# The second softmax's scores as eight small matmuls at once, and its transposes moved from TensorE to VectorE

## The chip, the cores and the metric

The kernel runs on one core of a Trainium2 chip. The metric is the device time of one launch, in microseconds, from runs of the same program. TensorE (PE in the profile; PEld is its weight load) writes only to PSUM. VectorE (DVE) and ScalarE (ACT) do the elementwise work, SyncE's queue (SP) starts most transfers and GpSimd's (POOL) a few. Each engine works through its own queue in order and waits at an instruction whose inputs or buffers aren't ready.

## The reference, cut to what matters

For 8 batches, 8 heads, 576 queries and keys of 64 values, and 32 packed rows per head:

```python
def sm_attn(qq, kk, vv):
    s = scale * np.matmul(qq, kk.transpose(0, 1, 3, 2))
    s = s - np.max(s, axis=-1, keepdims=True)
    a = np.exp(s)
    a = a / (np.sum(a, axis=-1, keepdims=True) + 1e-09)
    return np.matmul(a, vv)
p_packed = sm_attn(p, k, v)
out = sm_attn(q, p_packed, p_packed)
```

`out`, as 4608 tokens of 512 values, then goes through two MLPs with hidden size 2048. The first has a piecewise square as its nonlinearity, the second has SiLU. The change concerns the second `sm_attn`: its scores have 576 queries against 32 packed keys, per head, and its softmax runs over those 32.

## The kernel before, in words

The kernel is one program in two parts: attention with the first MLP (part A), then the second MLP (part B). Part A is a list of 256 steps, 32 for each of the 8 batches: 16 hidden blocks for each of the two halves (288 queries) of a batch. In each step TensorE does `a_h` for the step four ahead (line 569, six matmuls of 288 columns into one PSUM bank `ps_h`) and `a_y` for the step itself (line 604, twelve matmuls). Between them, over the steps in between, ScalarE makes `u` from `ps_h` (lines 578 and 579), VectorE limits it (`a_max`, line 584), ScalarE rounds it to `g` (line 588) and VectorE makes the rest of `g` (`a_lo`, line 594), one step ahead of the `a_y` that reads it. After the 16 steps of a half, `a_y`'s results are copied out by both (lines 613 and 616).

The output of the second softmax is not multiplied by the packed values on its own. The packed rows are multiplied into `w_in` first (`wp8`, line 497; `wp_out` casts it, lines 150 and 151), and `a_h` multiplies that with the softmax `a2`. So `a2`, with the (head, packed row) pairs on the partitions and queries along the free dimension, as a rounded part and a rest, is all that the second softmax has to deliver.

All work is put into one list of events with a key each, sorted, and emitted in that order, which is then the order of every engine's queue. Step i's `a_h` has key i + 0.3, its `a_y` i + 0.9, and the jobs of attention stand between them at i + 0.6. For batch b from 2 on, attention is done during the 32 steps of the batch before; the first of them is called `base` in the code. `front` (first softmax, packed rows) begins at `base` + 2, `back` (second softmax) at `base` + 14, `wp8` at `base` + 21, 25, 29 and 33, each with `wp_out` a step later. The new `a2` is wanted by `a_h` from `base` + 28 on.

`back` before: the 576 queries are taken as two tiles of 256 and one of 64, four steps apart. Each goes through six jobs, a step apart. `s2` (line 420) uses queries as weights, 64 at a time, and moves the 64 columns of packed keys of two heads: 16 matmuls, 4 for the last tile, which put queries on the partitions and the 32 packed rows of each head side by side. `s2_sub` (lines 431, 433) and `s2_norm` (446 to 449) are the softmax on VectorE around ScalarE's exponential `s2_exp` (438). `s2_tr` (457) turns the result with TensorE, against an identity, into PSUM, and `s2_out` (477, 479) splits it into `a2`.

Line 275 (`s1_8`) and line 286 (`s1_end8`) of `front`, and `wp8`, have a form that matters below: eight matmuls with 64 rows of contraction and 32 columns of weights, on eight tiles of TensorE's array, with 512 columns moving; results of the two heads of a pair go to two banks.

The preparation of the second MLP's weights is spread over the same steps: every 25 steps two conversions on VectorE (`conv_b`, lines 168 and 169) and then `a_first` to `a_fourth` (lines 651 to 660 with 151). For batch 4 (`base` 96) they fall on `base` + 17 and 19, and + 21 to 24.

The banks `ps_h`, `ps_s`, `ps_tr`, `ps_wp` come from one pool of four. Large SBUF tiles come from one pool, `big`, of 37.

Of the kernel before, what the change touches and what calls it, by code (L numbers as in the profile page):

```python
# [74 lines left out]

@with_exitstack
def attention_then_two_mlps(ctx: ExitStack, tc: tile.TileContext, kT, vv, qT, pT, w_in, w_out, w2_in, w2_out, out):

    nc = tc.nc
    B, P, NJ, S = kT.shape
    NP = pT.shape[3]
    D = P // 2
# [6 lines left out]
    HB = S // 2  # L102
    SC = S // P
    ST = S - SC * P
    NG = NJ // 2
# [8 lines left out]
    scale = 1.0 / float(D) ** 0.5  # L114

    const = ctx.enter_context(tc.tile_pool(name="const", bufs=1))
    big = ctx.enter_context(tc.tile_pool(name="big", bufs=37))
# [3 lines left out]
    a2_p = a2_s.enter_context(tc.tile_pool(name="a2_p", bufs=1))  # L121
    tc.swap_default_side()
    att = att_s.enter_context(tc.tile_pool(name="att", bufs=1))
# [10 lines left out]
    pb = const.tile([P, NJ, N2], F32, name="pbd")  # L134
# [11 lines left out]
    def bank(name):  # L146
        return ps_h.tile([P, 512], F32, tag="h", name=name)
# [6 lines left out]
    def words_of(raw):  # L154
        return raw.bitcast(U32).rearrange("p (n t) -> p n t", t=2)

    def to_f32_begin(raw):

        high = words_of(raw)[:, :, 1].bitcast(F32)
        nc.scalar.activation(high, high, AF.Prelu, scale=2.0 ** -112, alpha=-(2.0 ** 32))  # L162
# [25 lines left out]
    def conv_a(key):  # L188
        to_f32_begin(raw_t[key])
# [22 lines left out]
    kq_t, v_t, a2_t, wp_t = {}, {}, {}, {}  # L212
# [15 lines left out]
    def q_tiles(b):  # L228

        if b:  # L230
            return [[(2 * i * P, P), ((2 * i + 1) * P, P)] for i in range(SC // 2)] + [[(SC * P, ST)]]
        return [x for t in (0, HB) for x in ([(t, P), (t + P, P)], [(t + 2 * P, HB - 2 * P)])]

    def load_q(b, i):
        parts = q_tiles(b)[i]
        n = sum(x[1] for x in parts)
        if n > ST:
            t = big.tile([P, NJ, n], F32, tag="big", name="qt")
        else:
            t = att.tile([P, NJ, n], F32, tag="kqe", name="qte", bufs=2)  # L240
        nc.sync.dma_start(t, qT[b, :, :, parts[0][0]:parts[0][0] + n])
        kq_t["q", b, i] = t
# [9 lines left out]
    def att_jobs(b):  # L252


        st = {}
        pp = pp_t[b % 2]
# [148 lines left out]
        W2 = NJ * N2  # L405

        tiles = q_tiles(b)

        def s2(i):
# [53 lines left out]
        def s2_out(i):  # L463
# [14 lines left out]
            for hi, low, src in pieces:  # L478
                nc.vector.tensor_tensor(low, src, hi.bitcast(F32), op=ALU.subtract)

        def wp(f, g):
            ps = bank("ps_wp")
            w = w_in_t[g, f]
            for jj in range(2):
                nc.tensor.matmul(  # L485
                    ps[jj * N2:(jj + 1) * N2, :FW], pp[:, 2 * g + jj, :], w[:, jj, :], start=True, stop=True
                )
            st["wp", f, g] = ps
# [21 lines left out]
        def J(fn, *a):  # L510
            return lambda: fn(*a)
# [17 lines left out]
            [J(pp_out)],  # L529
        ]  # L530

        def back(every=4, only=None):
            which = range(len(tiles)) if only is None else only
            jobs = [[] for _ in range((len(which) - 1) * every + 6)]
            for n, i in enumerate(which):
                for k, fn in enumerate((s2, s2_sub, s2_exp, s2_norm, s2_tr, s2_out)):
                    jobs[n * every + k].append(J(fn, i))
            return jobs

        wps = [  # L540
            [[J(wp, f, g) for g in range(NG)] if b < 2 else [J(wp8, f)], [J(wp_out, f, g) for g in range(NG)]]
            for f in range(NF)
        ]
        return front, back, wps

    win_t = {}
# [74 lines left out]
    def load_part(b, t):  # L621
        for d in range(0, KD, 2):
            ysb = wk.tile([P, 2, HB], F32, tag="ysb", name="ysb", bufs=2)
            nc.sync.dma_start(ysb, y_dram[:, d:d + 2, t, b * HB:(b + 1) * HB])
            part_t["y", d // 2] = ysb

    def split_a(p, w, j, step):
# [168 lines left out]
                    s0 += m  # L804


    G = dict(pf1=4, pb1=18, w1=2, pf=2, pb=14, pw=21, lw=3, lk=4, lv=-1, lq=6, ai=34, ad=25, bev=4, oraw=1)
    starts = {b: (0,) if b else (0, KF // 2) for b in range(B)}
    steps = []
    for b in range(B):  # L810
# [6 lines left out]
    def ev(key, fn, *args):  # L817
        events.append((key, len(events), fn, args))

    def at(n, fn, *args):  # L820
        ev(n + 0.6, fn, *args)
# [4 lines left out]
    def slots(n, jobs, every=1):  # L826
        for i, slot in enumerate(jobs):
            for fn in slot:
                at(n + i * every, fn)

    with tc.manual_schedule():
# [3 lines left out]
        for _ in range(10):  # L835
            nc.tensor.matmul(warm[:, :P], ident, ident, start=True, stop=True)
        front, back, wps = att_jobs(0)

        def fill(n, own):
# [36 lines left out]
        def W(f, k, g):  # L876
            return (f"W{f}.{k}.{g}", wps[f][k][g])
# [67 lines left out]
        for g in range(NG):  # L945
            for k in range(2):
                n, fn = W(1, k, g)
                job(n, 2 + 0.1 * k + 0.01 * g, fn)
        for f in range(2, NF):
            for g in range(NG):  # L950
                for k in range(2):
                    n, fn = W(f, k, g)
                    job(n, 4 * f + k + 0.6, fn)
        for i, key in enumerate(ins[2 * KD:]):
            n = i + 3
# [54 lines left out]
        for p in range(NPR):  # L1010
            n = G['ai'] + G['ad'] * p
# [18 lines left out]
        for i in range(NBK):  # L1030
            n = kb(i * NPR)
# [92 lines left out]
```

## Time and profile before

| | |
|---|---|
| median of 3 runs | 1531.75 us (1530.99 to 1532.3) |
| span of the profiled execution | 1530.2 us |
| PE busy | 1512.8 us, 99% |
| PEld busy | 1380.4 us, 90% |
| DVE busy | 875.1 us, 57% |
| ACT busy | 743.4 us, 49% |
| POOL busy | 85.3 us, 6% |

The runs' time is that of the whole launch; the span runs from the first to the last instruction of one profiled execution. Busy times are shares of that span. Part A ends near 785 us.

### The profile page before, as it was taken

Reading aid. Unit: us, or ns where it says so; the run is one execution under the profiler, and the core shown is the slowest. Engines: PE = TensorE matmul, PEld = TensorE weight load, DVE = VectorE, ACT = ScalarE, POOL = GpSimd, SP = SyncE. Lnnn points to the kernel's source line nnn. Section 1 sums busy time; section 2 is a strip of 40 time slices with the busy share of each in tenths; the row PEclk is TensorE's granted clock in tenths of the full one; section 3 lists DMA queues with packets and bytes.
Section 4 is the critical chain, followed back from the end, with each engine's and each line's share of the span. In section 5 each row is a group of like instructions: output and inputs, shape, how many; then the busy total and the mean of one; then the engine's idle time right before and its main releaser. Section 6 shows DMA issues by size and latency. Waiting matters only on the chain.

```text
span 1530.2 us, 27671 instructions
## 1 busy us (share of the span) xinstructions
PE 1512.8 (99%) x10546; PEld 1380.4 (90%) x10546; DVE 875.1 (57%) x1831; ACT 743.4 (49%) x1665; POOL 85.3 (6%) x132
## 2 busy tenths in 40 slices
PE   8999999999999999999999999999999999999998
PEld 6788999989899899999998989999898989899997
DVE  5886565564746555575666664564364456447343
ACT  4775657565665656666754442343243334224232
POOL 1430000000000000000000010010001001001000
PEclk9999999999999999999999999999999999999999
DMA  9564545252445252432255653535444445445341
GB/s 333 178 222 141 187 132 169 100 166 102 139 157 169 89 182 70 167 116 92 99 179 187 214 165 108 175 122 161 138 137 146 136 147 160 123 151 173 103 138 62
DMA packets 136723, 226.99 MB, mean 148 GB/s; under 512 B 24336, under 2 KB 70416, under 8 KB 136592
## 3 DMA queue, kind: packets, MB, share of 16 engines
q1 hardware_dynamic: 127120, 192.19, 38.5%
q0 software_dynamic: 9472, 33.04, 6.6%
q8 instruction: 84, 1.38, 0.4%
q14 instruction: 47, 0.39, 0.1%
HBM read 186.25 MB, written 38.93 MB: 147 GB/s over the span
## 4 chain that ended last, share of the span: by engine, by line
PE 92%; DVE 2%; ACT 1%; issue 0%; DMA 0%; SPq 0%; DVEq 0%; ACTq 0%
PE ps_o L784 26%; PE ps_y L604 25%; PE ps_h L730 23%; PE ps_h L569 12%; PE ps_wp L497 2%; PE ps_s L420 2%; PE ps_pp L369 1%; PE ps_tr L457 1%; PE ps_wp L485 0%; DVE raw L168 0%; PE ps_s L275 0%; PE ps_et L334 0%; DVE w L169 0%; ACT u L578 0%; DVE u L584 0%
## 5 line engine op out<-in xcount | busy, mean ns | idle before, releaser
L604 PE MATMUL ps_y<-g,w_o 128*128 128x288 f32 x3072 | 459.8, 299 | 2.1 <-POOL g L594 1.8
L604 PEld LDWEIGHTS ps_y<-g,w_o 128*128 128x128 f32 x3072 | 421.3, 189 | 29.5 <-ACT u L578 15.1
L784 PE MATMUL ps_o<-w_o,g 128*128 128x512 f32 x1728 | 401.4, 390 | 0.0
L784 PEld LDWEIGHTS ps_o<-w_o,g 128*128 128x128 f32 x1728 | 324.1, 188 | 65.5
L730 PE MATMUL ps_h<-y,a2r 128*128 128x384 f32 x2016 | 362.6, 337 | 0.0
L730 PEld LDWEIGHTS ps_h<-y,a2r 128*128 128x128 f32 x2016 | 354.7, 188 | 3.7
L750 DVE TENSOR_TENSOR c<-ps_h,u 128x384 f32<-128x384 f32 x144 | 80.3, 558 | 313.0 <-PE ps_h L730 308.0
L756 ACT ACTIVATE s<-c 128x384 f32<-128x384 f32 x144 | 75.8, 526 | 370.1 <-DVE c L750 368.9
L584 DVE SCALAR_TENSOR_TENSOR u<-ps_h,u 128x288 f32<-128x288 f32 x256 | 116.5, 456 | 230.0 <-ACT u L579 229.7
L569 PE MATMUL ps_h<-a,wp 128*128 128x288 f32 x1536 | 245.0, 295 | 1.5 <-DVE u L584 0.6
L578 ACT ACTIVATE u<-ps_h,half 128x288 f32<-128x288 f32 x256 | 128.0, 500 | 206.4 <-PE ps_h L569 194.6
L569 PEld LDWEIGHTS ps_h<-a,wp 128*128 128x128 f32 x1536 | 217.1, 188 | 4.9 <-DVE u L584 1.5
L579 ACT ACTIVATE u<-u 128x288 f32<-128x288 f32 x256 | 113.8, 444 | 8.1
L765 ACT CAST g<-s 128x384 fp32r<-128x384 f32 x192 | 98.2, 512 | 32.2 <-DVE s L761 30.4
L594 DVE TENSOR_TENSOR g<-u,g 128x288 fp32r<-128x288 f32 x240 | 109.0, 454 | 1.4 <-ACT g L588 1.4
L588 ACT CAST g<-u 128x288 fp32r<-128x288 f32 x256 | 106.7, 418 | 2.5 <-PE ps_y L604 2.2
L770 DVE TENSOR_TENSOR g<-s,g 128x384 fp32r<-128x384 f32 x192 | 102.2, 553 | 4.8
L761 DVE TENSOR_TENSOR s<-c,s 128x384 f32<-128x384 f32 x144 | 79.1, 549 | 0.0
L803 POOL DMA_DIRECT2D out<-osb x40 | 21.4, 542 | 710.6 <-DVE osb L796 710.1
L553 POOL DMA_DIRECT2D win<-win_dram x48 | 25.7, 536 | 535.1 <-PE ps_wp L497 122.9
L151 DVE TENSOR_TENSOR wp<-ps_wp,wp 128x512 fp32r<-128x512 f32 x64 | 41.5, 685 | 10.7 <-ACT wp L150 10.4
L162 ACT ACTIVATE raw<-raw 128x512 f32<-128x512 f32 x64 | 42.7, 676 | 9.3 <-DMA raw<-w_out 5.5
(102 smaller groups left out, 942.1 us busy)
## 6 DMA issues: line engine op xcount, KB each, us to landing
a2r<-a_dram SPq DMA_DIRECT2D x336, 256.0 KB, 3.0
win<-win_dram POOLq DMA_DIRECT2D x48, 512.0 KB, 4.6
raw<-w_in SPq DMA_DIRECT2D x32, 512.0 KB, 7.9
raw<-w_out SPq DMA_DIRECT2D x32, 512.0 KB, 6.0
a_dram<-a2w SPq DMA_DIRECT2D x56, 256.0 KB, 3.3
y_dram<-ysb SPq DMA_DIRECT2D x36, 288.0 KB, 2.5
yr<-y_dram SPq DMA_DIRECT2D x24, 384.0 KB, 6.0
kt<-kT SPq DMA_DIRECT2D x16, 512.0 KB, 5.4
```

The costliest lines, as they stand in the source:

```text
L569: nc.tensor.matmul(ps[:, :HB], w[:, i, o:o + P], a2[:, k, g, :], start=(n == 0), stop=(n == 3 * NG - 1))
L578: nc.scalar.activation(u, h_ps[s][:, :HB], AF.Relu, bias=half, scale=0.5)
L579: nc.scalar.activation(u, u, AF.Square)
L584: nc.vector.scalar_tensor_tensor(u, h_ps.pop(s)[:, :HB], 1.0, u, op0=ALU.max, op1=ALU.min)
L588: nc.scalar.copy(g[:, 0], u_t[s])
L594: eng.tensor_tensor(g[:, 1], u_t.pop(s), g[:, 0].bitcast(F32), op=ALU.subtract)
L604: nc.tensor.matmul(acc["y"][d][:, :HB], w[:, i, d * P:(d + 1) * P], g[:, k], start=(first and n == 0), stop=(last and n == 2),)
L730: nc.tensor.matmul(ps, w[:, x, a * P:(a + 1) * P], y[:, k, :], start=(n == 0 and j in (0, 1, 3, 4)), stop=(n == 3 * KH - 1), skip_group_ch ...
L750: nc.vector.tensor_tensor(t, ps, sb[q, other], op=ALU.add)
L765: nc.scalar.copy(g[:, 0], c_t[q, name][0])
L770: nc.vector.tensor_tensor(g[:, 1], c_t.pop((q, name))[0], g[:, 0].bitcast(F32), op=ALU.subtract)
L784: nc.tensor.matmul(ps, g[:, x, c * P:(c + 1) * P], w[:, k, :], start=(first and (x, k) == PASSES[0]), stop=(last and (x, k) == PASSES[-1]),)
```

## The change

For batches 2 to 7 the second softmax goes another way; batches 0 and 1 are as before. `s2_8` uses packed keys as weights (64 rows by 32 columns) and moves 512 queries, eight matmuls on eight tiles of the array, two banks. `s2_end8` does the last 64 queries of all heads in one bank. The scores now have (head pair, packed row) on the partitions and queries along the free dimension. `t_in` lets VectorE turn each 32x32 block from PSUM into SBUF, after which the 32 packed rows of a head are side by side; `t_max`, `t_exp`, `t_norm` are the softmax as before; `t_out` turns the blocks back in SBUF, and `t_a2` splits that into `a2`. `back` begins two steps later (`base` + 16) and its jobs take ten steps instead of fourteen. q is loaded in two pieces of 512 queries and two head pairs each, six and five steps ahead, and one of 64 queries.

```diff
+    def load_q8(b, g):
+        if g == NG:
+            t = att.tile([P, NJ, ST], F32, tag="kqe", name="qte", bufs=2)
+            nc.sync.dma_start(t, qT[b, :, :, SC * P:])
+        else:
+            t = big.tile([P, 2, SC * P], F32, tag="big", name="qt")
+            nc.sync.dma_start(t, qT[b, :, 2 * g:2 * g + 2, :SC * P])
+        kq_t["q", b, g] = t
...
+        def s2_8():
+            banks = [bank("ps_s2") for _ in range(2)]
+            for j in range(NJ):
+                q = kq_t["q", b, j // 2] if j % 2 == 0 else kq_t.pop(("q", b, j // 2))
+                for e in range(2):
+                    rows, cols = slice(e * D, (e + 1) * D), slice(e * NP, (e + 1) * NP)
+                    nc.tensor.matmul(
+                        banks[e][j * NP:(j + 1) * NP, :SC * P], pp[rows, j, cols], q[rows, j % 2, :],
+                        start=True, stop=True, tile_position=(e * D, j * NP),
+                    )
+            st["s2", 0], st["s2", 1] = banks
+
+        def s2_end8():
...
+                    nc.tensor.matmul(
+                        ps[j * NP:(j + 1) * NP, e * ST:(e + 1) * ST], pp[:, j, e * NP:(e + 1) * NP], q[:, j, :],
+                        start=True, stop=True, tile_position=(0, j * NP),
+                    )
...
+        def t_in(i):
...
+            nc.vector.transpose(e2, st.pop(("s2", i))[:, :n])
...
+        def t_max(i):
+            e2 = blocks(i)
...
+            nc.vector.tensor_reduce(m2.rearrange("p a o -> p (a o)"), e2, axis=AX.X, op=ALU.max)
+            nc.vector.tensor_tensor(e2, e2, m2.to_broadcast([P, nh, NP]), op=ALU.subtract)
+
+        def t_exp(i):
+            e2 = st["e2", i]
+            nc.scalar.activation(e2, e2, AF.Exp, scale=scale)
+
+        def t_norm(i):
...
+            nc.vector.tensor_reduce(r2f, e2, axis=AX.X, op=ALU.add)
+            nc.vector.tensor_scalar_add(r2f, r2f, 1e-9)
+            nc.vector.reciprocal(r2f, r2f)
+            nc.vector.tensor_tensor(e2, e2, r2.to_broadcast([P, nh, NP]), op=ALU.mult)
+
+        def t_out(i):
...
+            nc.vector.transpose(st["e2t", i], st.pop(("e2", i)))
+
+        def t_a2(i):
...
+                a2, z2 = a2_t[b, 0][:, :, i, :], a2_t[b, 1][:, :, i, :SC * P - HB]
+                pieces = [(a2[:, 0], a2[:, 1], src[:, :HB]), (z2[:, 0], z2[:, 1], src[:, HB:])]
+            for hi, _, x in pieces:
+                nc.scalar.copy(hi, x)
+            for hi, low, x in pieces:
+                nc.vector.tensor_tensor(low, x, hi.bitcast(F32), op=ALU.subtract)
...
+        back8 = [
+            [J(s2_8)],
+            [J(t_in, 0), J(t_in, 1), J(s2_end8)],
+            [J(t_max, 0), J(t_in, 2)],
+            [J(t_exp, 0), J(t_max, 1)],
+            [J(t_norm, 0), J(t_exp, 1)],
+            [J(t_out, 0), J(t_norm, 1), J(t_max, 2)],
+            [J(t_a2, 0), J(t_out, 1), J(t_exp, 2)],
+            [J(t_a2, 1), J(t_norm, 2)],
+            [J(t_out, 2)],
+            [J(t_a2, 2)],
+        ]
...
         def back(every=4, only=None):
+            if b >= 2:
+                return back8
...
-    G = dict(pf1=4, pb1=18, w1=2, pf=2, pb=14, pw=21, lw=3, lk=4, lv=-1, lq=6, ai=34, ad=25, bev=4, oraw=1)
+    G = dict(pf1=4, pb1=18, w1=2, pf=2, pb=16, pw=21, lw=3, lk=4, lv=-1, lq=6, ai=34, ad=25, bev=4, oraw=1)
...
         def plan_back(b, n):
+            if b >= 2:
+                for g in range(NG + 1):
+                    at(n - G['lq'] + min(g, 1), load_q8, b, g)
+                slots(n, jobs[b][1]())
+                return
```

Line numbers in the rows of the changed kernel's order are its own: L486 is `s2_8`, L497 `s2_end8`, L575 `wp8`, L662 `a_h`, L697 `a_y`, L511 `t_in`, L521 and L522 `t_max`, L533 to L536 `t_norm`, L541 `t_out`, L677 `a_max`, L687 `a_lo`, L557 the rest in `t_a2`, L140 the rest in `wp_out` and in the weights' preparation, L737 in `a_first`, L745 and L746 in `a_second`.

TensorE's queue before, in batch 4, from step `base` + 18 on: the transposes of the first query tile and the scores of the second (`s2(1)`), between an `a_h` and an `a_y`.

```order
L569 MATMUL ps_h<-a_3947,wp_1_4058 128x288 x3
L569 MATMUL ps_h<-a_3947,wp_1_4061 128x288 x3
L457 MATMUL ps_tr<-ident,e_4835 128x128 x4
L420 MATMUL ps_s_4946<-pp_88,qt 64x2x32 x16
L604 MATMUL ps_y<-g,w_o_409 128x288 x12
```

TensorE's queue of the changed kernel, in batch 4, at steps `base` + 16 and 17: `s2_8` and, a step later, `s2_end8`.

```order
L662 MATMUL ps_h<-a_3863,wp_1_4017 128x288 x3
L486 MATMUL ps_s_4808<-qt,pp_88 32x512
L486 MATMUL ps_s_4809<-qt,pp_88 32x512
...
L697 MATMUL ps_y<-g,w_o_424 128x288 x12
L662 MATMUL ps_h<-a_3863,wp_1_4014 128x288 x3
L662 MATMUL ps_h<-a_3863,wp_1_4017 128x288 x3
L497 MATMUL ps_s2e<-qte,pp_88 32x64 x8
L697 MATMUL ps_y<-g,w_o_393 128x288 x12
```

What stood in four steps (+14, +18, +22, +26) now stands in two, and no transposition of this softmax is left on TensorE.

VectorE's queue before, in batch 4, at step `base` + 21: `a_lo` and `a_max` of that step, the normalization of the second tile, and behind it `a_first`.

```order
L594 TENSOR_TENSOR g<-u,g 128x288
L584 SCALAR_TENSOR_TENSOR u<-ps_h,u 128x288
L446 TENSOR_REDUCE r_5057<-e_4999 128x16
L447 TENSOR_SCALAR r_5057<-r_5057 128x16
L448 RECIPROCAL r_5057<-r_5057 128x16
L449 TENSOR_TENSOR e_4999<-e_4999,r_5057 128x512
L651 TENSOR_TENSOR s_5072<-w 128x256
```

VectorE's queue of the changed kernel at the same step.

```order
L687 TENSOR_TENSOR g<-u,g 128x288
L677 SCALAR_TENSOR_TENSOR u<-ps_h,u 128x288
L541 STREAM_TRANSPOSE e2t<-e_4849 128x512
L533 TENSOR_REDUCE r_4994<-e_4851 128x16
L534 TENSOR_SCALAR r_4994<-r_4994 128x16
L535 RECIPROCAL r_4994<-r_4994 128x16
L536 TENSOR_TENSOR e_4851<-e_4851,r_4994 128x512
L521 TENSOR_REDUCE m_4999<-e2r 128x4
L522 TENSOR_TENSOR e2r<-e2r,m_4999 128x128
L737 TENSOR_TENSOR s_5012<-w 128x256
```

Between the step's `a_max` and `a_first` there now stand a transposition and the maximum of the last 64 queries as well.

VectorE's queue of the changed kernel one step later, at `base` + 22, where four such pieces meet: `t_a2(0)`, `t_out(1)`, `wp_out` and `a_second`.

```order
L687 TENSOR_TENSOR g<-u,g 128x288
L677 SCALAR_TENSOR_TENSOR u<-ps_h,u 128x288
L557 TENSOR_TENSOR a_5046<-e2t,a_5046 128x288
L557 TENSOR_TENSOR a_5047<-e2t,a_5047 128x224
L541 STREAM_TRANSPOSE e2t<-e_4851 128x512
L140 TENSOR_TENSOR wp_0_5055<-ps_wp_5002,wp_0_5055 128x512
L140 TENSOR_TENSOR wp_0_5058<-ps_wp_5003,wp_0_5058 128x512
L745 TENSOR_TENSOR w<-w 128x256
L746 TENSOR_TENSOR w<-w,s_5012 128x256
L140 TENSOR_TENSOR a2w<-w,a2w 128x256
```

Before, this step had of the softmax nothing: only `wp_out` and `a_second` stood behind its `a_max`.

## Rows read from the trace of the kernel before

**Rows 1.** Busy us, share of the span, number of instructions: PE and DVE.

```profile
PE 1512.8 (99%) x10546; PEld 1380.4 (90%) x10546; DVE 875.1 (57%) x1831; ACT 743.4 (49%) x1665; POOL 85.3 (6%) x132
```

**Rows 2.** The chain that ended last, by engine.

```profile
PE 92%; DVE 2%; ACT 1%; issue 0%; DMA 0%; SPq 0%; DVEq 0%; ACTq 0%
```

**Rows 3.** Timeline of PE, batches 4 and 5: start us, us, instruction, count.

```profile
433.87 0.43 PE L286 MATMUL ps_s1e<-kte,pbd 128*32 128x64 f32 x16
434.23 1.85 PE L604 MATMUL ps_y<-g,w_o 128*128 128x288 f32 x12
...
465.46 0.96 PE L569 MATMUL ps_h<-a,wp 128*128 128x288 f32 x6
...
469.54 0.96 PE L569 MATMUL ps_h<-a,wp 128*128 128x288 f32 x6
...
476.73 0.96 PE L569 MATMUL ps_h<-a,wp 128*128 128x288 f32 x6
...
481.87 0.96 PE L569 MATMUL ps_h<-a,wp 128*128 128x288 f32 x6
...
486.66 0.96 PE L569 MATMUL ps_h<-a,wp 128*128 128x288 f32 x6
487.55 1.09 PE L497 MATMUL ps_wp<-win,pp 64*32 64x512 f32 x16
488.56 1.85 PE L604 MATMUL ps_y<-g,w_o 128*128 128x288 f32 x12
490.25 0.96 PE L569 MATMUL ps_h<-a,wp 128*128 128x288 f32 x6
...
493.90 0.96 PE L569 MATMUL ps_h<-a,wp 128*128 128x288 f32 x6
...
502.26 0.96 PE L569 MATMUL ps_h<-a,wp 128*128 128x288 f32 x6
...
505.13 0.96 PE L569 MATMUL ps_h<-a,wp 128*128 128x288 f32 x6
```

**Rows 4.** Timeline of PE, batch 6, around the same two jobs.

```profile
569.07 0.96 PE L569 MATMUL ps_h<-a,wp 128*128 128x288 f32 x6
...
573.59 0.96 PE L569 MATMUL ps_h<-a,wp 128*128 128x288 f32 x6
```

**Rows 5.** Timeline of DVE, batches 4 and 5; in brackets idle time and releaser.

```profile
389.64 0.68 DVE L431 TENSOR_REDUCE m<-ps_s 128x16 f32<-128x512 f32 x1
390.36 0.69 DVE L433 TENSOR_TENSOR e<-ps_s,m 128x512 f32<-128x512 f32 x1
390.97 0.42 DVE L168 TENSOR_SCALAR raw<-raw 128x512 uint32<-128x512 uint32 x1
...
392.03 0.45 DVE L594 TENSOR_TENSOR g<-u,g 128x288 fp32r<-128x288 f32 x1
...
394.32 0.68 DVE L446 TENSOR_REDUCE r<-e 128x16 f32<-128x512 f32 x1
...
396.13 0.42 DVE L651 TENSOR_TENSOR s<-w 128x256 f32<-128x256 f32 x1
...
397.53 0.45 DVE L594 TENSOR_TENSOR g<-u,g 128x288 fp32r<-128x288 f32 x1
...
398.27 1.28 DVE L151 TENSOR_TENSOR wp<-ps_wp,wp 128x512 fp32r<-128x512 f32 x2
...
400.46 0.45 DVE L594 TENSOR_TENSOR g<-u,g 128x288 fp32r<-128x288 f32 x1
...
492.26 0.46 DVE L584 SCALAR_TENSOR_TENSOR u<-ps_h,u 128x288 f32<-128x288 f32 x1 [1.13 <-ACT u L579]
```

**Rows 6.** Instructions grouped by line and shape: busy us, mean ns, idle time before.

```profile
L208 POOL TENSOR_TENSOR w_o<-w,w_o 128x512 fp32r<-128x512 f32 x16 | 22.3, 1397 | 59.0 <-ACT w_o L206 48.9 <-PE ps_h L569 7.1 <-DMA ysb<-y_dram 2.8
```

**Rows 7.** Transfers: KB each, median us from issue to landing.

```profile
qt<-qT SPq DMA_DIRECT2D x16, 512.0 KB, 8.2
```

More of the change, by code (lines that the diff above doesn't have):

```diff
@@ L479, in s2_out @@
                 nc.vector.tensor_tensor(low, src, hi.bitcast(F32), op=ALU.subtract)
+        NB = SC * P // NP
+        def s2_8():
[9 more added lines that the diff above has]
+            st["s2", 0], st["s2", 1] = banks
@@ new lines, in s2_end8 @@
+        def s2_end8():
+            q = kq_t.pop(("q", b, NG))
+            ps = bank("ps_s2e")
+            for e in range(2):
+                for j in range(NJ):
+                    nc.tensor.matmul(
+                        ps[j * NP:(j + 1) * NP, e * ST:(e + 1) * ST], pp[:, j, e * NP:(e + 1) * NP], q[:, j, :],
+                        start=True, stop=True, tile_position=(0, j * NP),
+                    )
+            st["s2", 2] = ps
+        def t_in(i):
+            if i == 2:
+                both = att.tile([P, 2, 2 * ST], F32, tag="ett", name="e2r")
+                e2, back_ = both[:, 0], both[:, 1]
+                st["e2t", i] = back_
+            else:
+                e2 = att.tile([P, SC * P], F32, tag="e2", name="e2", bufs=2)
+            n = 2 * ST if i == 2 else SC * P
+            nc.vector.transpose(e2, st.pop(("s2", i))[:, :n])
+            st["e2", i] = e2
@@ new lines, in blocks @@
+        def blocks(i):
+            return st["e2", i].rearrange("p (h n) -> p h n", n=NP)
+        def t_max(i):
+            e2 = blocks(i)
+            nh = e2.shape[1]
+            m2 = att.tile([P, 16, 1], F32, tag="m2", name="m2", bufs=2)[:, :nh]
+            nc.vector.tensor_reduce(m2.rearrange("p a o -> p (a o)"), e2, axis=AX.X, op=ALU.max)
[3 more added lines that the diff above has]
+            nc.scalar.activation(e2, e2, AF.Exp, scale=scale)
@@ new lines, in t_norm @@
+        def t_norm(i):
+            e2 = blocks(i)
+            nh = e2.shape[1]
+            r2 = att.tile([P, 16, 1], F32, tag="m2", name="r2", bufs=2)[:, :nh]
+            r2f = r2.rearrange("p a o -> p (a o)")
+            nc.vector.tensor_reduce(r2f, e2, axis=AX.X, op=ALU.add)
[3 more added lines that the diff above has]
+        def t_out(i):
+            if i < 2:
+                st["e2t", i] = att.tile([P, SC * P], F32, tag="et", name="e2t", bufs=2)
+            nc.vector.transpose(st["e2t", i], st.pop(("e2", i)))
@@ new lines, in t_a2 @@
+        def t_a2(i):
+            src = st.pop(("e2t", i))
+            for t in range(2):
+                if (b, t) not in a2_t:
+                    a2_t[b, t] = a2_p.tile([P, 2, NG, HB], F32R, tag="a2", name="a2", bufs=3)
+            if i == 2:
+                a2 = a2_t[b, 1][:, :, :, SC * P - HB:]
+                pieces = [(a2[:, 0], a2[:, 1], src.rearrange("p (e t) -> p e t", e=2))]
+            else:
+                a2, z2 = a2_t[b, 0][:, :, i, :], a2_t[b, 1][:, :, i, :SC * P - HB]
[4 more added lines that the diff above has]
+                nc.vector.tensor_tensor(low, x, hi.bitcast(F32), op=ALU.subtract)
```

## The prediction

> **What bounds the kernel now.** I read the shares of busy time first, then the chain that ended last, then TensorE's timeline in the stretch that the change touches, then VectorE's order of work there. PE is busy for 1512.8 of 1530.2 us, VectorE for 57% [rows 1]; the chain that ended last lies on PE for 92% and on DVE for 2% [rows 2]. So a microsecond of PE's queue that disappears in this stretch is a microsecond of span, unless another queue makes PE wait in its place.
>
> The timeline [rows 3] shows how regular PE is there. I count from the start of one step's a_h (L569, six matmuls) to the start of the next; I write "step n" for the n-th step after a batch's `base`. Two bare steps take 486.66 − 481.87 = 4.79 us, 2.39 each. Whatever stands between an a_h and its a_y makes that step longer, and the surplus over 2.39 is the full price of the insertion, with what it costs to enter and leave it. VectorE meanwhile waits for ScalarE's `u`, which waits for PE: at 492.26 it had idled 1.13 us for it, 2.01 us after the a_h of that step began at 490.25 [rows 3, 5]. It keeps pace with PE; it doesn't set it.
>
> **What is removed on PE**, per batch, by that reading of [rows 3]: s2(0) 469.54 − 465.46 − 2.39 = 1.69; s2_tr(0) with s2(1) 481.87 − 476.73 − 2.39 = 2.75; s2_tr(1) with the short s2(2) 493.90 − 490.25 − 2.39 = 1.26; s2_tr(2) 505.13 − 502.26 − 2.39 = 0.48. The second is unusually long in batch 5, which these rows are of: the transpose waits there for VectorE's normalization, and so it does in batch 4. In batch 6 it is 573.59 − 569.07 − 2.39 = 2.13 [rows 4], as in batches 2, 3 and 7. Sum over six batches: 6 × (1.69 + 1.26 + 0.48) + 4 × 2.13 + 2 × 2.75 = 20.6 + 8.5 + 5.5 = 34.6 us.
>
> **What is added on PE.** s2_8 has the form of wp8 and s1_8, which the kernel has already: eight matmuls of 64 rows by 32 columns on eight array tiles, 512 columns moving. A wp8 step is 490.25 − 486.66 = 3.59 us, so an insertion of 1.20, of which the block itself is 488.56 − 487.55 = 1.01 and entering and leaving 0.19 [rows 3]. s2_end8 has the form of s1_end8, 434.23 − 433.87 = 0.36, but stands alone in its step and so pays entry too: 0.36 to 1.20 as the ends, 0.55 taken. Six times 1.75 is 10.5 us. On PE alone the change gives 34.6 − 10.5 = 24.1 us.
>
> The page "TensorEngine Tiling (Array Packing)" of the Trainium skill, under PSUM Bottleneck, says that tiling speeds TensorE up but not the emptying of PSUM, which may become the bottleneck. That speaks against this change, and the trace can't refute it ahead, since VectorE's queue gets longer; it stands beside the first and third rival.
>
> **What is added on VectorE.** Per batch four block transposes of 128x512 and two of 128x128; the tail's four operations shrink from 64x256 to 128x128; one cast piece and one subtraction piece more. No row shows a transpose. The cheapest 128x512 operation on DVE takes 0.42 us (shift, L168), the one that is nearest, because it reads its 128x512 f32 from PSUM and writes SBUF, 0.69 (L433), with its follower 0.61 behind it; GpSimd's tensor_tensor of that size takes 1.40 [rows 5, 6]. I take 0.61 as the room that one takes in the queue, with 0.42 and 1.40 as ends, and 0.25 for a small one, an estimate somewhat above a quarter of 0.61. That is some 2.5 us more per batch and 15 in all on an engine that is busy for 57%; the sum is no problem, the place may be.
>
> The page "VectorE: DVE Perf Modes" of the Trainium skill, under The three transpose paths, has 311 ns for a 128x128 bf16 block transpose on VectorE, against 390 ns on TensorE. At 0.31 for the small ones the sum would move by under 0.1 us a batch; no row of the trace has the operation.
>
> PE waits for VectorE in two ways: a_y needs the `g` that a_lo finishes, one step ahead of it in VectorE's queue, and a_h, s2 and wp take the four PSUM banks in turn, which a_max, t_in and wp_out empty. The softmax chain itself is wanted only at step 28, when a_h of the next batch begins; it ends at step 25. So I follow VectorE's queue with zero at the start of step 16's a_h. PE then starts step 17 at 3.6 (2.39 + 1.20), 18 at 6.5, 19 at 8.9, 20 at 11.3, 21 at 13.7, 22 at 17.3 (a wp8 stands in 21), 23 at 19.7, 24 at 22.1, 25 at 24.5. Room in VectorE's queue by differences of starts [rows 5]: t_max as reduce and subtract 390.97 − 389.64 = 1.33; one weight conversion (conv_b) 392.03 − 390.97 = 1.06; t_norm 396.13 − 394.32 = 1.81; a_first 397.53 − 396.13 = 1.40; a_lo and a_max 398.27 − 397.53 = 0.74; two wp subtractions with a_second 400.46 − 398.27 = 2.19, 1.2 and 1.0.
>
> - An ordinary batch: in step 17 ScalarE comes from the copies at the half's end, a_max ends near 3.0 and t_in at 4.2. From then on `u`, 2.0 after the a_h before, is ready at 5.6, 8.5 and 10.9 for the a_max of steps 18, 19 and 20, where the queue arrives at 4.6, 7.9 and 10.6: it waits 1.9 us in all, and step 20's a_max ends at 11.3. Then t_norm(0): 13.1. Step 21: 0.74, t_out(0) 0.61, t_norm(1) 1.81, t_max(2) 0.5: 16.8. Step 22: 0.74, t_a2(0) 0.68, t_out(1) 0.61, wp_out 1.2: 20.0. The a_lo for step 24's a_y: 20.4. PE wants it at 22.1 + 0.8 = 22.9. Spare: 2.5 us, no stall. Batch 7 has a conversion in steps 21 and 23, which fits into that.
> - Batch 4 has conversions in steps 17 and 19 (ScalarE's part ahead of them makes t_in 0.4 later), a_first in 21, a_second in 22. t_in ends at 4.6, step 17 at 5.7, 18 at 8.0, 19 at 11.1, 20 at 13.7, 21 at 13.7 + 3.7 + 1.40 = 18.8, 22 at 18.8 + 3.2 + 1.0 = 23.0, that a_lo at 23.4: 0.5 late. The rest of step 23 with a_third takes 2.5, step 24's two 0.74, 26.7, when the bank for step 25's second wp8 half comes free; PE wants it near 25.9: 0.8 more. In sum some 1.3 us; 1.5 taken.
>
> ScalarE: three exponentials as before with a shorter tail, a2 casts in five pieces for four, so at most 0.2 us a batch more, hidden in its waits for PE, which are of the kind that VectorE shows; uncovered it would be 1.2 us. SP: the same bytes of q in three transfers, two 512 KB tiles asked for six and five steps (14 and 12 us) ahead; such a tile takes 8.2 us from issue to landing [rows 7]. If that cover were gone, each batch would pay what is late.
>
> **Sum.** 24.1 − 1.5 = 22.6 us less. The profiled execution's span was 1530.2 us and the runs' median 1531.75, so 1.5 lies around the span and stays. 1531.75 − 22.6 = 1509.1 us.
>
> **Rivals.**
> 1. *VectorE's burst in steps 20 to 23 makes PE wait more than that, and some gain is lost.* With transposes at 1.40: in ordinary batches t_in's 1.6 more goes into the 1.9 of waiting before step 20, t_out's 1.6 into the spare 2.5; batch 7 comes about 1 late, batch 4 4.5. Then 24.1 − 5.5 = 18.6: 1513. For it: the DVE jobs are packed one step apart where they lay over fourteen steps, and PE already waited for this chain in batches 4 and 5. Against: no DVE row of this size reaches 1.4.
> 2. *Nothing changes*, because a transfer or another engine sets the step: 1531.7. Against it: bare steps take 2.39 us with PE's matmuls end to end, and VectorE idles behind PE.
> 3. *Slower: block transposes of 32-bit data are several times as dear as any row here.* With e more than 0.61 for each, an ordinary batch stalls by 4e − (1.9 + 2.5); this passes the gain of 4.0 a batch at e = 2.1, so from some 2.7 us a transpose on. At 3.2 us: 4 × 2.6 − 4.4 = 6.0 in each of six batches, 1531.75 − 24.1 + 36 = 1543.7. For it: no trace of this kernel has the operation. Against: it reads and writes one stream, as the copies and casts do.
>
> The rule on the PSUM bottleneck, from the page of the Trainium skill named above ("TensorEngine Tiling (Array Packing)"), would give the first or the third, by the price that emptying PSUM has here.
>
> **Numbers.** Forecast 0.78 (1505 to 1513), first rival 0.12, second 0.03, third 0.07. The range is 1505 to 1516: the lower end has no stall and 0.36 for s2_end8 (1506.5), and 1.5 us below that for what two decimals hide; the upper the first rival and 3 us of waits that I can't see. A measurement tells some 0.2% (3 us) from no change; faster 0.90, the same 0.03, slower 0.07.
>
> **What would show it.** On PE, six insertions near 1.2 us (s2_8) and six near 0.55 (s2_end8), none of transposes of the second softmax after batch 1; each batch some 4 us shorter; no wait of PE's for DVE outside batch 4, and there in steps 23 to 25. On DVE, transposes of 0.6 to 0.8 us. I am wrong if transposes pass 1.4 us, or if PE waits in steps 18 to 25 of every batch, for a bank or for `g`.

## The result, and the profile after

The changed kernel takes 1508.65 us (median; 1508.3 to 1509.8) where the kernel before, measured beside it, takes 1531.37: a ratio of 0.9856, with a 95% interval of 0.9842 to 0.987. The medians differ by 22.7 us, or 1.5%. The forecast was 1509.1.

Busy time and the chain that ended last, after, answer to [rows 1, 2]. PE is busy for 22.5 us less and is still the bound; VectorE has 8.6 us more.

```profile
PE 1490.3 (99%) x10246; PEld 1356.2 (90%) x10246; DVE 883.7 (59%) x1873; ACT 744.5 (49%) x1671; POOL 84.8 (6%) x132
PE 92%; DVE 2%; ACT 1%; issue 1%; DMA 0%; SPq 0%; DVEq 0%; ACTq 0%
```

The prediction put 15 us more on VectorE. Its busy time rose by 8.6, because busy time counts an overlap once: in a full queue the next record begins some 0.08 us before the one ahead ends (a t_out from 384.15 for 0.70, its follower from 384.77). The single durations, added up over the trace, rose by 14.8 us (955.8 to 970.6).

The timeline of PE in batch 6, where [rows 3, 4] showed the old insertions, begins with step 16's a_h. Line numbers are the changed kernel's: L486 is s2_8, L497 s2_end8, L662 a_h, L697 a_y.

```profile
547.02 0.96 PE L662 MATMUL ps_h<-a,wp 128*128 128x288 f32 x6
547.90 1.09 PE L486 MATMUL ps_s<-qt,pp 64*32 64x512 f32 x16
548.92 1.85 PE L697 MATMUL ps_y<-g,w_o 128*128 128x288 f32 x12
550.62 0.96 PE L662 MATMUL ps_h<-a,wp 128*128 128x288 f32 x6
551.50 0.43 PE L497 MATMUL ps_s2e<-qte,pp 128*32 128x64 f32 x16
...
553.56 0.96 PE L662 MATMUL ps_h<-a,wp 128*128 128x288 f32 x6
```

Read from a_h to a_h: 550.62 − 547.02 − 2.39 = 1.21 for s2_8 and 553.56 − 550.62 − 2.39 = 0.55 for s2_end8. In batches 2, 3, 5, 6 and 7 every other step has the length it has without the softmax (2.38 to 2.40, and 3.60 with a wp8). From the a_h of one batch's step 14 to that of the next batch, beginning with batch 2, it was 91.72, 91.76, 92.32, 92.34 and 91.72 us; it is 87.97, 87.96, 89.50, 87.97 and 87.97. The third interval, batch 4's, is the exception, and the only one.

The operations that no row of before had, grouped by line and shape (mean ns behind the comma): L511 is t_in, L541 t_out.

```profile
L541 DVE STREAM_TRANSPOSE e2t<-e 128x512 f32<-128x512 f32 x12 | 8.4, 701 | 0.0
...
L511 DVE STREAM_TRANSPOSE e<-ps_s 128x512 f32<-128x512 f32 x12 | 7.8, 689 | 0.0
...
L511 DVE STREAM_TRANSPOSE e2r<-ps_s2e 128x128 f32<-128x128 f32 x6 | 1.9, 308 | 0.0
L541 DVE STREAM_TRANSPOSE e2r<-e2r 128x128 f32<-128x128 f32 x6 | 1.8, 300 | 0.0
```

A block transpose of 128x512 takes 0.70 us from SBUF and 0.69 from PSUM, as L433's subtraction did [rows 5]; a small one 0.31. The page "VectorE: DVE Perf Modes" of the Trainium skill, under The three transpose paths, has 311 ns for the 128x128 one in bf16. The trace is close to it with 300 to 308 ns, but in f32; no run here has bf16.

Where batch 4 waits, on PE: steps 22 to 25.

```profile
386.88 0.96 PE L662 MATMUL ps_h<-a,wp 128*128 128x288 f32 x6
...
389.34 1.06 PE L662 MATMUL ps_h<-a,wp 128*128 128x288 f32 x6
...
391.85 0.96 PE L662 MATMUL ps_h<-a,wp 128*128 128x288 f32 x6
392.65 0.29 PE L697 MATMUL ps_y<-g,w_o 128*128 128x288 f32 x1
393.17 1.75 PE L697 MATMUL ps_y<-g,w_o 128*128 128x288 f32 x11 [0.23 <-DVE g L687]
394.76 0.96 PE L662 MATMUL ps_h<-a,wp 128*128 128x288 f32 x6
395.65 1.92 PE L575 MATMUL ps_wp<-win,pp 64*32 64x512 f32 x16
...
399.20 0.96 PE L662 MATMUL ps_h<-a,wp 128*128 128x288 f32 x6
```

The same place by the weight loads (PEld), where a wait for data or a bank shows as a gap, and below it VectorE's instructions that end those waits.

```profile
393.17 1.52 PEld L697 LDWEIGHTS ps_y<-g,w_o 128*128 128x128 f32 x11 [0.47 <-DVE g L687]
...
396.48 0.18 PEld L575 LDWEIGHTS ps_wp<-win,pp 64*32 64x32 f32 x14 [0.70 <-DVE u L677]
```

```profile
392.67 0.45 DVE L687 TENSOR_TENSOR g<-u,g 128x288 fp32r<-128x288 f32 x1
...
395.98 0.45 DVE L677 SCALAR_TENSOR_TENSOR u<-ps_h,u 128x288 f32<-128x288 f32 x1
```

Step 24 has 394.76 − 391.85 = 2.91 us: its a_y does one matmul and then waits for the a_lo of 392.67, because the rest of `g` comes later than the rounded part. Step 25 has 399.20 − 394.76 = 4.44 where 3.60 is the rule: two of wp8's matmuls start, into the bank that is free, and the other bank is freed only by the a_max of 395.98. Steps 22 and 23 lose 0.1 each. In sum 1.5 us.

### The profile page after: what moved, and what is told of

It is laid out like the page before. It is cut to its first block, busy times and chain, and to the rows that moved or that the text cites. A ratio compares the mean times of both kernels' runs of the same rounds, so it can differ in the third digit from the quotient of the medians.

```text
span 1506.7 us, 27109 instructions
## 1 busy us (share of the span) xinstructions
PE 1490.3 (99%) x10246; PEld 1356.2 (90%) x10246; DVE 883.7 (59%) x1873; ACT 744.5 (49%) x1671; POOL 84.8 (6%) x132
## 4 chain that ended last, share of the span: by engine, by line
PE 92%; DVE 2%; ACT 1%; issue 1%; DMA 0%; SPq 0%; DVEq 0%; ACTq 0%
PE ps_o L870 26%; PE ps_y L697 26%; PE ps_h L816 23%; PE ps_h L662 12%; PE ps_wp L575 2%; PE ps_pp L366 1%; PE ps_wp L563 0%; DVE raw L156 0%; PE ps_s L486 0%; PE ps_s L272 0%; PE ps_et L331 0%; DVE w L157 0%; DVE g L687 0%; DVE u L677 0%; DVE w_in L157 0%
## 5 line engine op out<-in xcount | busy, mean ns | idle before, releaser
L697 PE MATMUL ps_y<-g,w_o 128*128 128x288 f32 x3072 | 458.0, 298 | 1.9 <-POOL g L687 1.3
L697 PEld LDWEIGHTS ps_y<-g,w_o 128*128 128x128 f32 x3072 | 420.9, 188 | 33.5 <-ACT u L671 13.4
L662 PE MATMUL ps_h<-a,wp 128*128 128x288 f32 x1536 | 245.2, 295 | 1.5 <-DVE u L677 0.6
L677 DVE SCALAR_TENSOR_TENSOR u<-ps_h,u 128x288 f32<-128x288 f32 x256 | 116.2, 455 | 205.5 <-ACT u L672 205.2
L662 PEld LDWEIGHTS ps_h<-a,wp 128*128 128x128 f32 x1536 | 217.1, 188 | 5.1 <-DVE u L677 1.5
L687 DVE TENSOR_TENSOR g<-u,g 128x288 fp32r<-128x288 f32 x240 | 108.5, 452 | 1.4 <-ACT g L681 1.4
L681 ACT CAST g<-u 128x288 fp32r<-128x288 f32 x256 | 106.7, 418 | 2.5 <-PE ps_y L697 2.3
L140 DVE TENSOR_TENSOR wp<-ps_wp,wp 128x512 fp32r<-128x512 f32 x64 | 41.3, 680 | 8.3 <-ACT wp L139 8.1
```

Source lines behind the costliest of these rows:

```text
L662: nc.tensor.matmul(ps[:, :HB], w[:, i, o:o + P], a2[:, k, g, :], start=(n == 0), stop=(n == 3 * NG - 1))
L677: nc.vector.scalar_tensor_tensor(u, h_ps.pop(s)[:, :HB], 1.0, u, op0=ALU.max, op1=ALU.min)
L681: nc.scalar.copy(g[:, 0], u_t[s])
L687: eng.tensor_tensor(g[:, 1], u_t.pop(s), g[:, 0].bitcast(F32), op=ALU.subtract)
L697: nc.tensor.matmul(acc["y"][d][:, :HB], w[:, i, d * P:(d + 1) * P], g[:, k], start=(first and n == 0), stop=(last and n == 2),)
```

## The experiments

The questions: do the terms on PE add up as reckoned, one by one; is batch 4's loss the meeting of two jobs in VectorE's queue; and how much room does that queue have. The rival to the whole reading is that VectorE, or the place, or the loads, carries part of the gain. Times of before beside them are 1530.6 to 1531.3 us. The loads of q have no run of their own; in neither trace does PE wait for a transfer of q in batches 2 to 7.

**The turning alone.** In the kernel before, `s2_tr` for batches 2 to 7 becomes:

```diff
         def s2_tr(i):
+            if b >= 2:
+                e2 = st.pop(("e2", i)).rearrange("p h n -> p (h n)")
+                rows, nch = part2(i)
+                t = att.tile([P, SC * P], F32, tag="et", name="e2t", bufs=2)
+                for x in range(2):
+                    if rows == P:
+                        nc.vector.transpose(t[:, :nch * W2], e2)
+                    else:
+                        nc.vector.transpose(t[x * rows:(x + 1) * rows, :P], e2[:, x * P:(x + 1) * P])
+                st["tr", i] = t
+                return
```

> The kernel before with only its second-softmax transposes of batches 2 to 7 taken from TensorE; the scores stay as they were (queries as weights). In place of each set of TensorE transposes, VectorE does two block transposes (two of 128x512 for a large tile, two of 64x128 for the last), as many as the change adds. That changes what is computed: a block transpose doesn't turn the whole 128x128 tile, so the softmax reaches the first MLP with its entries permuted; its time alone is of interest. Theory (what counts is PE's queue): s2_tr costs 2.13 - 1.69 = 0.44 in its first place, about the same in the second, 0.48 in the third, 1.36 us a batch, 8.2 in six, and the waits of batches 4 and 5 for the normalization go (1.2): 1531.4 - 9.4 = 1522 us. The other 14.7 us of the 24.1 would be the scores' new form. Rival (most of the gain is the transposes and their dependency on the softmax): 1512 us or less. Rival (VectorE's load eats it up): 1531 us.

Measured: 1523.85 us, 7.4 less than before and 1.9 above what was expected; both rivals (1512 and 1531) are far off. In an ordinary batch the steps that held s2_tr came down by 0.43, 0.46 and 0.47 us, 1.36 in all as expected (a batch takes 90.38 us for 91.72), and the waits for the normalization are gone. Batch 4 got a new wait of 0.8 us, at s2(2), for a bank that a_max (L595 here; L580 is a_h) empties behind the longer queue:

```profile
393.75 0.96 PE L580 MATMUL ps_h<-a,wp 128*128 128x288 f32 x6
395.42 0.68 PE L420 MATMUL ps_s<-pp,qte 128*64 128x64 f32 x8 [0.71 <-DVE u L595]
```

From batch 2's step 14 to the last a_h the trace is 8.5 us shorter than before's (569.4 for 577.9), as 9.4 less 0.8 would have it. The other 1 us that the medians lack lies outside these steps, where runs of all kernels differ by that much.

**The scores alone.** `s2_8`, `s2_end8` and the new loads, with TensorE's transposes kept:

```diff
...
+                return [
+                    [J(s2_8)],
+                    [J(s2_sub, 0), J(s2_sub, 1), J(s2_end8)],
+                    [J(s2_exp, 0), J(s2_sub, 2)],
+                    [J(s2_exp, 1), J(s2_norm, 0)],
+                    [J(s2_norm, 1), J(s2_exp, 2)],
+                    [J(s2_tr, 0)],
+                    [J(s2_out, 0), J(s2_norm, 2)],
+                    [J(s2_tr, 1)],
+                    [J(s2_out, 1)],
+                    [J(s2_tr, 2)],
+                    [J(s2_out, 2)],
+                ]
...
```

> The new form of the scores alone: s2_8, s2_end8 and the new loads of q as in the change, at base + 16, but no block transposes; the softmax runs on the scores as they lie and TensorE's transposes stay (four of 128x128 for each bank and one for the last queries, each two steps or more behind its normalization). That leaves out the turning into rows of 32, so that the softmax is taken over 32 queries in place of 32 packed rows; its time alone is of interest. Theory (PE's queue decides, and the terms add up): per batch 1.20 and 0.55 for the scores, 0.5, 0.65 and 0.3 for three sets of transposes, 3.2 in place of 5.5, six times 2.3 and the waits of batches 4 and 5 (1.2): 1531 - 15 = 1516 us, within 2. Rival (the eight-tile form is only worth anything together with the turning on VectorE): 1525 us or more.

Measured: 1513.98 us, 2.0 below what was expected. An ordinary batch takes 88.93 us, 2.79 less than before. The direction and the two scores' terms are as expected (3.60 and 2.94 for their steps), the transposes were put too dear. In batch 6 (L623 is a_h here, L497 the transposes):

```profile
564.23 0.96 PE L623 MATMUL ps_h<-a,wp 128*128 128x288 f32 x6
565.03 0.60 PE L497 MATMUL ps_tr<-ident,e 128*128 128x128 f32 x4
...
568.30 0.96 PE L623 MATMUL ps_h<-a,wp 128*128 128x288 f32 x6
...
570.69 0.96 PE L623 MATMUL ps_h<-a,wp 128*128 128x288 f32 x6
...
573.53 0.96 PE L623 MATMUL ps_h<-a,wp 128*128 128x288 f32 x6
```

Step 21 has 4.07 (3.60 without the transposes), step 23 has 573.53 − 570.69 = 2.84 us, and the third set added 0.11 to step 25: 1.04 in all, for 1.45. With 1.04 of transposes taken away from 88.93, 87.89 is left, and the changed kernel has 87.97. So in this order the parts add up: some 2.8 us a batch from the scores' form, 1.0 from the transposes that would still stand beside them. They aren't independent, though: beside the old scores the same transposes cost 1.34, so the two gains taken singly (2.79 and 1.34) come to 0.4 more than the 3.75 of both. Batch 4 waits in this run too, 0.6 us for a bank at step 21's wp8 (4.68 for 4.07), without any block transpose.

**The place alone.** `pb=14` becomes `pb=16` in the kernel before.

> The kernel before with its second softmax begun two steps later (base + 16 for base + 14), as the change does; nothing else. Theory: the place has nothing to do with the gain; the insertions cost the same on PE, only the waits for the normalization in batches 4 and 5 (0.6 us each) may come or go: 1531.4, within 2 us. Rival (the later start avoids the half's end and is part of the gain): 3 us or more faster, 1528 us or less.

Measured: 1529.53 us, ratio 0.9988 (0.9979 to 0.9998). All batches take 91.69 us: the waits of batches 4 and 5 (0.6 each) are gone, and no other step that holds a job changed by more than 0.03. The medians differ by 1.7 us, 0.5 more than these waits; that is within the runs' scatter. Those 1.2 us were counted among the change's; a shift by two steps would have given them too.

**The transposes twice, and four times.**

```diff
-            nc.vector.transpose(e2, st.pop(("s2", i))[:, :n])
+            ps = st.pop(("s2", i))[:, :n]
+            for _ in range(2):
+                nc.vector.transpose(e2, ps)
...
-            nc.vector.transpose(st["e2t", i], st.pop(("e2", i)))
+            e2 = st.pop(("e2", i))
+            for _ in range(2):
+                nc.vector.transpose(st["e2t", i], e2)
```

> The changed kernel with each of VectorE's block transposes of batches 2 to 7 done twice, the second time over the same result; nothing else. Theory (PE sets the pace, VectorE's queue has 1.9 us of waiting before step 20 and 2.5 us spare at step 24's a_y in an ordinary batch): the 1.2 us more at steps 17 and 18 and the 1.2 us more at steps 21 and 22 vanish in batches 2, 3, 5 and 6; batch 7 waits some 1 us, batch 4's wait of 1.5 us grows to about 4.2. So 1508.7 + 3.7 = 1512.4 us, with unchanged step lengths (2.39) in batches 2, 3, 5 and 6. Rival (VectorE already holds PE up all along, and each added piece of VectorE work shows): 2.9 us a batch, 1526 us, in every batch.

Measured: 1514.27 us, 5.6 more than the change. Batches 2, 3 and 6 kept every step; batch 5, expected to keep them too, lost 0.4, batch 7 1.4 and batch 4 another 3.3, to 4.85 in all. The pattern is the expected one but for batch 5, and the sum was put 1.9 too small. Of batch 4's 4.85 the wait itself is 2.65; 1.62 came in the step after it and 0.58 in step 25. PE there (L666 is a_h, L701 a_y, L681 a_max), and its clock by windows (us, PE busy, granted clock, DMA share, GB/s):

```profile
386.80 0.96 PE L666 MATMUL ps_h<-a,wp 128*128 128x288 f32 x6
...
391.85 1.61 PE L666 MATMUL ps_h<-a,wp 128*128 128x288 f32 x6 [2.49 <-DVE u L681]
...
395.86 0.96 PE L666 MATMUL ps_h<-a,wp 128*128 128x288 f32 x6
```

```profile
389.00:392.00 3.00, 0.51 (x4) 1.00 0.00 0
392.00:396.00 4.00, 4.00 (x20) 0.57 0.39 131
```

The wait for a bank adds 2.65 us to step 22. After it PE ran at a granted clock of 0.57, mostly its lower level, and step 23 took 4.01 us for 2.39.

> The changed kernel with each block transpose of batches 2 to 7 done four times over the same result; nothing else. Theory: 3.7 us more at t_in, 0.7 at the small one, 3.7 at t_out. An ordinary batch then waits 3.7 + 0.7 - 1.9 + 3.7 - 2.5 = 3.7 us, batch 7 about 6 and batch 4 about 9.6, in sum 30 us less the 1.5 that is there: 1537 us, which is slower than the kernel before (1531.4), so that the sign turns between two and four transposes' worth. Rival (the spare room is much larger, since a late a_lo can be made good over the whole batch): under 1520 us. Rival (all added work shows): 8.5 us a batch, 1560 us.

Measured: 1553.95 us, slower than before (1.0148, 1.0133 to 1.0163). The sign turned between two and four, as expected, but by 45 us more than the change and not 29. By the time alone the rival in which all added work shows (1560) is nearer than the expectation (1537), so the batches have to decide. Batches 2, 3, 5 and 6 lost 5.8 to 7.4 us, not 3.7. One cause is in VectorE's queue of batch 3: L513 is t_in, L545 t_out, L691 a_lo, L535 the reduction in t_norm.

```profile
291.96 5.81 DVE L513 STREAM_TRANSPOSE e<-ps_s 128x512 f32<-128x512 f32 x8
297.69 0.42 DVE L691 TENSOR_TENSOR g<-u,g 128x288 fp32r<-128x288 f32 x1
...
306.30 2.94 DVE L545 STREAM_TRANSPOSE e2t<-e 128x512 f32<-128x512 f32 x4
309.17 0.64 DVE L535 TENSOR_REDUCE r<-e 128x16 f32<-128x512 f32 x1
```

Eight took 5.73 us and four 2.87: 0.72 for each on average, not 0.61. Taken singly, a repeat starts 0.71 to 0.75 us after the transpose before it, which reads and writes the same two tiles; what stands behind the last repeat starts after 0.64. That makes t_in's extra 5.73 − 1.23 = 4.5, the small one's 1.1 and t_out's 2 × (2.87 − 0.62) = 4.5, and 10.1 − 4.4 = 5.7 us by the prediction's own formula of the spare room. Batch 6, which has no preparation of weights in these steps, measured 93.81 − 87.97 = 5.8; had all of the added work shown, it would have lost 10.1 or more. Batches 3 and 5 lost 6.2 and 7.1, which isn't taken apart here; batch 2 lost 7.4, and there PE's clock is a further cause (below). So the room of some 4.4 us stands; the price of the repeated operation was wrong.

**The other job out of the way.** In the changed kernel:

```diff
-            n = G['ai'] + G['ad'] * p
+            n = G['ai'] + G['ad'] * p + (6 if p == 3 else 0)
```

> The changed kernel with the fourth pair of second-MLP weights (loads, conversions, a_first to a_fourth) prepared six steps later, so that in batch 4 the two conversions fall on steps 23 and 25 and a_first to a_fourth on 27 to 30, behind the softmax's burst. Theory (batch 4's wait of 1.5 us is the meeting of the two in VectorE's queue): steps 22 to 25 of batch 4 take 2.40, 2.40, 2.40 and 3.60 as in the other batches, 1508.7 - 1.5 = 1507.2 us. Rival (the wait comes from the banks, which the softmax and the packed rows take whatever VectorE has behind them): batch 4 keeps its longer steps, 1508.7 us.

Measured: 1507.43 us (ratio 0.985). Batch 4 takes 87.97 us like the others, 1.53 less, with steps 22 to 25 at 2.40, 2.39, 2.40 and 3.60. Its softmax and its packed rows take the same banks in the same order, so what was late was VectorE, through a_first, a_second and the two conversions: in the changed kernel its queue shows no wait from 372.82 to 398.69. The medians moved by 1.2 us, and by 0.5 measured against before in the same session; at this size the trace tells more than they do.

**The last queries in the same step.** In the changed kernel:

```diff
-            [J(s2_8)],
-            [J(t_in, 0), J(t_in, 1), J(s2_end8)],
+            [J(s2_8), J(s2_end8)],
+            [J(t_in, 0), J(t_in, 1)],
```

> The changed kernel with s2_end8 moved into the step of s2_8, behind it. Theory (an insertion costs its block plus 0.19 us for entering and leaving, once for a step): six times 0.19 less, 1508.7 - 1.1 = 1507.6 us; the joined step takes 3.95 us, the next 2.39. Rival (three banks at once leave too few of the four for a_h): the next a_h waits 0.5 us or more in each batch, 1511 us or more.

Measured: 1508.66 us, no gain. The joined step takes 4.07 to 4.11 us, not 3.95. In batch 6, s2_8 on PE, the weight loads of s2_end8, and on VectorE the a_max that they wait for:

```profile
547.48 1.09 PE L486 MATMUL ps_s<-qt,pp 64*32 64x512 f32 x16
```

```profile
548.61 0.27 PEld L497 LDWEIGHTS ps_s2e<-qte,pp 128*32 128x32 f32 x16 [0.95 <-DVE u L677]
```

```profile
548.10 0.46 DVE L677 SCALAR_TENSOR_TENSOR u<-ps_h,u 128x288 f32<-128x288 f32 x1 [0.89 <-ACT u L672]
```

s2_8 had ended its turn at 547.48 + 1.02 = 548.50, the a_max ends at 548.56, and s2_end8 begins at 548.61. Ordinary batches take 87.83 to 87.91 us for 87.97, so 0.06 to 0.14 of the expected 0.19 a batch was left, too little for the medians to show.

> The two edits together: s2_end8 in the step of s2_8, and the fourth pair of weights six steps later. Theory: the two are independent, 1508.7 - 1.5 - 1.1 = 1506.1 us, faster than the kernel before and the changed one. Rival (one of them brings a new wait): no faster than the better of the two alone, 1507.2 us.

Measured: 1506.63 us (ratio 0.9843, 0.9828 to 0.9858); 0.8 less than the better of the two alone, and by the trace, from batch 2's step 14 to the last a_h, 553.4 for 554.2.

**One step later.** The same with `pb=17`:

> The version with s2_end8 joined to s2_8 and the fourth pair of weights six steps later, with the second softmax of batches 2 to 7 begun one step later (base + 17). At base + 16 the joined block lost 0.11 us before s2_end8, in the step in which VectorE comes late from the copies at the half's end. Theory (s2_end8's bank is that of an a_h which VectorE empties too late there): one step on, the bank is free, the joined step takes 3.95 us in place of 4.07 to 4.10, six times 0.12 less: 1506.6 - 0.7 = 1505.9 us. Rival (0.11 us is what TensorE needs to change from eight array tiles to four): the joined step stays at 4.07, 1506.6 us.

Measured: 1505.92 us, ratio 0.9839 (0.9825 to 0.9854), the lowest median of all, and faster than both kernels of this case. The 0.7 us to the run before are within the scatter of the two (1505.8 to 1506.8 and 1506.3 to 1506.8). What tells is the trace, in batch 6:

```profile
547.94 1.09 PE L486 MATMUL ps_s<-qt,pp 64*32 64x512 f32 x16
548.96 0.43 PE L497 MATMUL ps_s2e<-qte,pp 128*32 128x64 f32 x16
```

s2_end8 now follows without a gap, 1.02 behind s2_8's start, in every batch, and the joined step takes 3.95. The 0.11 us was the bank and not a change of tiling. Over a whole batch 0.06 of it is left: 87.77 us for 87.83.

## Why the prediction was right

**The bound.** PE's queue. That held: each part's gain is what its own insertions left in PE's queue, with the place worth nothing beyond the 1.2 us of two waits. That the loads are worth nothing is read from the traces and not from a run.

**What PE loses and gains.** 1.20 and 0.55 were taken for the new blocks; 1.21 and 0.55 were measured, and 3.75 us per ordinary batch for the reckoned 3.8. The 0.55 wasn't derived where it stands, but it is the block's 0.36 and the 0.19 for entering and leaving it.

**VectorE's price.** 0.61 us of room for a block transpose of 512 columns, from the nearest row: t_in's two took 374.43 − 373.20 = 1.23. The ends (0.42, 1.40) weren't needed.

```profile
373.20 1.30 DVE L511 STREAM_TRANSPOSE e<-ps_s 128x512 f32<-128x512 f32 x2
374.43 0.38 DVE L156 TENSOR_SCALAR raw<-raw 128x512 uint32<-128x512 uint32 x1
```

A small one took 0.23 us of the queue for 0.25. With 0.31 in its place the sum moves by 2 × 0.06 = 0.12 us a batch, and not by under 0.1; nothing hangs on that.

**An ordinary batch.** In batch 6, zero at 547.02, VectorE waits for `u` in steps 18, 19 and 20, and then gets step 24's a_lo done in time:

```profile
552.62 0.46 DVE L677 SCALAR_TENSOR_TENSOR u<-ps_h,u 128x288 f32<-128x288 f32 x1 [0.88 <-ACT u L672]
...
555.56 0.46 DVE L677 SCALAR_TENSOR_TENSOR u<-ps_h,u 128x288 f32<-128x288 f32 x1 [0.60 <-ACT u L672]
...
557.97 0.46 DVE L677 SCALAR_TENSOR_TENSOR u<-ps_h,u 128x288 f32<-128x288 f32 x1 [0.26 <-ACT u L672]
...
567.03 0.43 DVE L687 TENSOR_TENSOR g<-u,g 128x288 fp32r<-128x288 f32 x1
```

That is 1.74 us of waiting for the 1.9 predicted, and an a_lo that ends at 567.46 − 547.02 = 20.4, as predicted, 2.5 us before PE wants it.

**Batch 4.** The ledger of VectorE's queue, zero at step 16's a_h (369.55), against the starts in the trace:

| end of | predicted | measured |
|---|---|---|
| t_in | 4.6 | 4.9 |
| step 18 | 8.0 | 8.2 |
| step 19 | 11.1 | 11.3 |
| step 20 | 13.7 | 13.9 |
| step 21 | 18.8 | 18.9 |
| step 22 | 23.0 | 23.1 |
| bank for step 25's wp8 | 26.7 | 26.9 |

0.5 us late at step 24's a_y and 0.84 at step 25's wp8 are 0.5 and 0.8 in the prediction; the total of 1.5 is what moving the preparation gave back in batch 4's trace (1.53). The prediction reckoned 1.3 and took 1.5 without a term for the rest: that steps 22 and 23 lost just these 0.2 is luck. Other batches didn't wait, batch 7 neither.

**The rivals.** The first, a burst that costs more, didn't come; with each transpose twice it began to, and in batches 4, 5 and 7 only. The second, no change, is excluded by the interval. The third needs more than twice the price: with four in place of one the kernel is slower than before. The page "TensorEngine Tiling (Array Packing)" of the Trainium skill, under PSUM Bottleneck, says that after a fourfold speedup of TensorE by tiling the copies out of PSUM may become the bottleneck. The trace agrees for batch 4 in part: 0.84 of its 1.5 us is a wait for a bank, and 0.5 is one for `g`, which isn't PSUM. In an ordinary batch some 4.4 us of VectorE's room lie before it.

The span fell by 23.5 us, the median by 22.7. Of the span's difference 0.8 lies ahead of the first changed step (189.66 and 188.83 us for batch 2's step 14), and the other runs scatter there as well (188.6 to 189.3), so it isn't the change's. From there to the last a_h it is 577.91 and 555.68 us, so the six batches gave 22.2; the last 0.5 lies behind that, where runs scatter by 1.4. Measured against 22.2, PE's terms were 0.3 us too high (23.8 with batch 4's 1.5 put back, for 24.1). That forecast and median agree within 0.5 us is in part luck.

## What to carry to other kernels

Where one engine's queue is full, price an insertion by the surplus of its step over a bare one, entry and exit with it; the length of the block alone (1.02 us for s2_8) would have missed 0.19 us at each. Then write down the queue of the engine that takes the work over, step by step, with starts and not durations, and look for the one batch in which another periodic job falls on the same steps. Here moving that job gave back its whole loss, 1.5 us in the trace; a smaller burst wasn't tried.

## What was not expected of the hardware

A block transpose of 128x512 that repeats the one before it starts 0.71 to 0.75 us after it, where other work starts 0.60 to 0.64 us after a transpose. The repeat reads and writes the same tiles as the one before; which of the two holds it back, no run here shows.

PE's clock can fall after a wait of 2.5 to 3.1 us, and need not. It fell after the 2.49 us with each transpose twice. With four transposes, PE waited 3.12 us for a bank in batch 2 and 3.13 in batch 3. By windows (us, PE busy, granted clock, DMA share, GB/s):

```profile
212.00:217.00 5.00, 1.88 (x15) 1.00 0.15 59
217.00:221.00 4.00, 3.45 (x18) 0.68 0.00 0
221.00:225.00 4.00, 3.94 (x16) 0.50 0.00 0
225.00:229.00 4.00, 4.00 (x38) 0.96 0.00 0
308.00:312.00 4.00, 1.22 (x10) 1.00 0.11 43
312.00:316.00 4.00, 2.65 (x18) 1.00 0.00 0
```

In batch 2 PE fell to the lower level (0.50 of 2.4 GHz) for some 7 us after it, in batch 3 it stayed at 1.00. In batches 5 and 6 it fell after waits of 3.13 and 3.12 us, in 4 and 7 with waits of 4.58 and 4.20. What tells batch 3 apart stays open. A fall can make a long wait dearer than its length, which the ledger doesn't hold: step 24 took 4.4 us in batch 2, and 2.5 in batch 3. It need not: batch 6 had its fall in step 23 (0.50 from 601 to 604), and its steps 23 and 24 were as long as those of batch 3, in which PE, at the full clock, waited 1.46 us for a bank at the end of step 23.
